# The h stage of the last 896 tokens with seven block products in place of eight

## The chip, the cores and the metric

The kernel runs on one core of a Trainium2 chip. The metric is the device time of one execution in microseconds; before the change it is 640.79 us, the median of three runs (639.9, 643.55, 640.79). PE is the matmul engine, DVE, ACT and POOL are the vector, scalar and GpSimd engines, SP issues the DMAs.

## The reference

Causal attention over 4 batches, 12 heads, 448 positions, head size 64, and on its output x (1792 tokens of 768) an MLP with a squared relu:

```python
scores = scale * np.matmul(q, k.transpose(0, 1, 3, 2))
scores = np.where(mask, -1000000000.0, scores)
attn = np.exp(scores - np.max(scores, axis=-1, keepdims=True))
attn = attn / (np.sum(attn, axis=-1, keepdims=True) + 1e-09)
x = (attn @ v).transpose(0, 2, 1, 3).reshape(B * S, H * D)
h = np.maximum(x @ w_in, 0.0)          # w_in  768 x 2048
return (h * h @ w_out)                 # w_out 2048 x 768
```

The weights arrive as 8-byte words, and everything else as f32.

## The kernel before, in words

Tokens are worked off in two halves of 896 (two batches each, `ph` 0 and 1). For a half, the 2048 columns of h are taken in four groups (`gr`) of four blocks of 128 (`GF`). A group has an h stage and an o stage. The h stage has eight units (`h_unit`, block f, batch h of the half): 6 blocks c of the 768 inputs, and for each of them three matmuls of 128 x 128 weights by 448 tokens, since every operand is held as a high and a low half (f32r) and hi*hi + hi*lo + lo*hi is summed in PSUM (lines 490 to 492). ACT then applies the relu from PSUM into a tile `r`, the square is taken, and `split` makes its two halves g (lines 240 to 250). The o stage has 14 units (`o_unit`, 7 token blocks by 2 column halves) of 4 x 3 matmuls of 384 columns (lines 526 to 528), added by DVE to `acc`; after the last group SP stores `acc` to the output (line 544).

Weights come in pieces (`piece`), 6 of w_in and 8 of w_out per group and half: SP loads 8-byte words into one of three `raw` tiles (line 467), two ACT, a shift, an addition and a combining instruction on DVE (lines 475, 243, 478) make an f32 in a `z` tile, and `split` writes a high half (ACT or POOL) and a low half (DVE or POOL) into `wi` or `wo`. All of this is done in both halves of the tokens.

Attention runs per pair of heads, 12 pairs for each half of the tokens (`attention`): scores (line 327), a masked maximum on DVE (340), exp on ACT (344), normalisation on POOL (353), transposes (367) and the product with v (387) on PE. The pairs of the second half of the tokens run between the MLP matmuls of the first half; their result goes to `x_dram` (line 435), and in the last o stage of the first half `again` loads the twelve blocks back (591) and splits them into the x tiles.

The order of the work is written by a planner (`Plan`). Every piece of work is an `op` with a rank, the engines that could do it with an assumed duration, what it reads and writes, and the buffers that it takes and drops. `emit` simulates the engines: it picks again and again the op that could start first (the rank decides between equals), and writes the instructions in the order of their simulated start. So each engine, and SP's DMA queue, has one fixed order; in the run an instruction waits for its data and buffers, and all behind it on that engine wait with it.

## Time and profile before

| what | value |
|---|---|
| median of three runs | 640.79 us (639.9 to 643.55) |
| profiled execution, span from first to last instruction | 638.4 us |
| what the median has above that span | 2.39 us |
| PE busy | 619.2 us (97%) |
| DVE, POOL, ACT busy | 450.4 (71%), 395.8 (62%), 356.7 us (56%) |
| DMA | 78.61 MB, mean 123 GB/s |

The profile is of one execution, whose time outside the span is not shown. "Busy" of PE adds up matmuls whose modelled ends overlap the next start, so a matmul's cost is read from the distance between starts. Engine names stand before lines of the kernel (L526 is line 526); operations recorded in a helper have the helper's line, so that tiles tell them apart.

### The profile page before, as it was taken

How to read it: one execution, taken by the hardware profiler on the slowest of the kernel's cores; microseconds unless marked ns; L12 is line 12 of the kernel's file. 1: busy time of each engine (PE TensorE's matmuls, PEld its weight loads, DVE VectorE, ACT ScalarE, POOL GpSimd, SP SyncE). 2: the span in 40 equal slices, each digit the busy share in tenths (PEclk: the TensorE clock that was granted, in tenths of full speed). 3: DMA queues.
4: the chain of work that ended last, by engine and by line, in shares of the span. 5: the costliest groups of instructions: out<-in, count | busy, mean ns of one | idle time of the engine just before them, and what ended most of it. 6: DMA issues, size and time to landing. Idle time of an engine off the chain costs nothing.

```text
span 638.4 us, 11482 instructions
## 1 busy us (share of the span) xinstructions
PE 619.2 (97%) x3936; PEld 544.8 (85%) x3936; DVE 450.4 (71%) x911; ACT 356.7 (56%) x856; POOL 395.8 (62%) x498
## 2 busy tenths in 40 slices
PE   3999999999999999999999999999999999999997
PEld 2666777798888898789888889999999999999997
DVE  5789865686668787678885479759845993897022
ACT  4789977676787456675557553545653344333300
POOL 1567854775678655767576688876657556656410
PEclk9799999999999999999999999999999999999999
DMA  9898931545574546544463258723541453141022
GB/s 156 158 201 150 186 80 31 109 154 152 118 173 130 151 98 155 152 96 115 126 159 100 77 164 248 210 73 109 158 130 34 108 155 101 59 123 50 1 87 87
DMA packets 134779, 78.61 MB, mean 123 GB/s; under 512 B 113729, under 2 KB 120385, under 8 KB 134721
## 3 DMA queue, kind: packets, MB, share of 16 engines
q1 hardware_dynamic: 131008, 77.42, 47.2%
q10 hardware_dynamic: 3712, 0.46, 0.5%
q8 instruction: 31, 0.51, 0.3%
q14 instruction: 28, 0.22, 0.1%
HBM read 69.60 MB, written 8.26 MB: 122 GB/s over the span
## 4 chain that ended last, share of the span: by engine, by line
PE 84%; DVE 5%; DMA 3%; POOL 3%; ACT 2%; issue 1%; SPq 0%; DVEq 0%; POOLq 0%; ACTq 0%
PE ps L526 12%; PE ps L527 12%; PE ps L528 12%; PE ps L490 11%; PE ps L491 11%; PE ps L492 11%; PE ps L387 6%; PE ps L367 5%; PE ps L327 4%; POOL ap L353 3%; DVE ps L340 2%; DMA v<-in_v_dram 1%; DMA bq<-in_q_dram 1%; ACT ap L344 1%; DMA aq<-in_q_dram 1%
## 5 line engine op out<-in xcount | busy, mean ns | idle before, releaser
L526 PE MATMUL ps<-wo,g 128*128 128x384 f32 x448 | 153.2, 342 | 0.0
L527 PE MATMUL ps<-wo,g 128*128 128x384 f32 x448 | 151.2, 338 | 0.0
L528 PE MATMUL ps<-wo,g 128*128 128x384 f32 x448 | 151.2, 337 | 0.0
L490 PE MATMUL ps<-x,wi 128*128 128x448 f32 x384 | 145.0, 378 | 0.6 <-ACT x L240 0.6
L491 PE MATMUL ps<-x,wi 128*128 128x448 f32 x384 | 140.6, 366 | 0.2 <-DVE x L243 0.2
L492 PE MATMUL ps<-x,wi 128*128 128x448 f32 x384 | 140.5, 366 | 0.0
L240 ACT ACTIVATE b<-raw 128x384 int32<-128x384 uint32 (+1 forms) x112 | 68.3, 610 | 89.1 <-DVE z L243 80.3
L243 DVE CUSTOM_DVE_ANT_0 z<-z,b 128x768 uint16<-128x768 uint16 (+1 forms) x112 | 102.9, 919 | 8.8 <-ACT b L240 1.9
L478 DVE SCALAR_TENSOR_TENSOR z<-raw,z 128x384 int32<-128x384 int32 (+1 forms) x112 | 94.8, 846 | 2.9
L353 POOL TENSOR_SCALAR ap<-ap,asm 128x448 f32<-128x448 f32 (+6 forms) x123 | 71.5, 600 | 35.1 <-DVE asm L411 21.8
L340 DVE CUSTOM_DVE_ANT_0 ps<-ps,mask 128x448 f32<-128x448 f32 (+6 forms) x168 | 68.8, 443 | 33.9 <-PE ps L327 24.9
L240 ACT ACTIVATE z<-raw 128x384 f32<-128x384 f32 (+1 forms) x112 | 67.8, 609 | 32.6 <-POOL wi L247 15.6
L526 PEld LDWEIGHTS ps<-wo,g 128*128 128x128 f32 x448 | 84.2, 188 | 1.4 <-issue 1.0
L527 PEld LDWEIGHTS ps<-wo,g 128*128 128x128 f32 x448 | 84.2, 188 | 0.1
L528 PEld LDWEIGHTS ps<-wo,g 128*128 128x128 f32 x448 | 84.1, 188 | 0.0
L490 PEld LDWEIGHTS ps<-x,wi 128*128 128x128 f32 x384 | 72.2, 188 | 9.0 <-issue 1.7
L475 DVE TENSOR_SCALAR z<-z 128x384 int32<-128x384 int32 (+1 forms) x112 | 63.3, 565 | 23.3 <-ACT z L240 23.0
L243 DVE TENSOR_TENSOR acc<-ps,acc 128x384 f32<-128x384 f32 x84 | 46.0, 550 | 46.1 <-PE ps L528 45.8
L492 PEld LDWEIGHTS ps<-x,wi 128*128 128x128 f32 x384 | 72.1, 188 | 6.1
L491 PEld LDWEIGHTS ps<-x,wi 128*128 128x128 f32 x384 | 72.2, 188 | 5.8 <-DVE x L243 0.5
L344 ACT ACTIVATE ap<-ps,mx 128x448 f32<-128x448 f32 (+6 forms) x126 | 58.7, 481 | 14.3 <-DVE mx L340 13.9
L247 POOL TENSOR_TENSOR g<-r,g 128x448 fp32r<-128x448 f32 x52 | 64.9, 1249 | 2.4
(65 smaller groups left out, 848.3 us busy)
## 6 DMA issues: line engine op xcount, KB each, us to landing
raw<-in_moe_w_in_dram SPq DMA_DIRECT2D x48, 512.0 KB, 3.9
raw<-in_moe_w_out_dram SPq DMA_DIRECT2D x64, 384.0 KB, 3.4
out_dram<-acc SPq DMA_DIRECT2D x28, 192.0 KB, 2.5
v<-in_v_dram SPq DMA_DIRECT2D x24, 192.0 KB, 4.0
ak<-in_k_dram SPq DMA_DIRECT2D x72, 56.0 KB, 2.7
aq<-in_q_dram SPq DMA_DIRECT2D x68, 56.0 KB, 2.6
x_dram<-xs SPq DMA_DIRECT2D x12, 224.0 KB, 3.8
xs<-x_dram SPq DMA_DIRECT2D x12, 224.0 KB, 2.7
```

The source lines that it names most:

```text
L240: return (ACT, t_act(n, psum, more), lambda: nc.scalar.activation(dst(), src(), func, **kw))
L243: return (DVE, t_dve(n) + more, lambda: nc.vector.tensor_tensor(out=dst(), in0=a(), in1=b(), op=op))
L340: plan.op(at, [(DVE, t_dve(w), lambda: nc.vector.tensor_tensor_reduce(out=at_(), in0=at_(), in1=mask[:, S - w:], scale=-SCALE, scalar=3.0e ...
L344: plan.op(at, [(ACT, t_act(w, True, 0.5), lambda: nc.scalar.activation(probabilities(c), at_(), AF.Exp, bias=mx.t, scale=-1.0, accum_out=s ...
L353: (POOL, 0.0005 * CW[c] + 0.34, lambda: nc.gpsimd.tensor_scalar(*operands(), 1.0, op0=ALU.mult, op1=ALU.mult)),
L478: plan.op(rank - 2, [(DVE, t_dve(n) + 0.2, lambda: nc.vector.scalar_tensor_tensor(out=z(), in0=word(1), scalar=-2 ** 31, in1=z(), op0=ALU. ...
L490: nc.tensor.matmul(o, w[:, 0], x[:, 0], start=c == 0, stop=False)
L491: nc.tensor.matmul(o, w[:, 0], x[:, 1], start=False, stop=False)
L492: nc.tensor.matmul(o, w[:, 1], x[:, 0], start=False, stop=c == NP - 1)
L526: nc.tensor.matmul(res(), g[:, 0], w[:, 0], start=f == 0, stop=False)
L527: nc.tensor.matmul(res(), g[:, 0], w[:, 1], start=False, stop=False)
L528: nc.tensor.matmul(res(), g[:, 1], w[:, 0], start=False, stop=f == GF - 1)
```

## The change

In the second half of the tokens the h stage is computed by Strassen's scheme. The weights of two blocks f1, f2 are cut in two along the 768 inputs (3 blocks each), and x in two along the inputs and in two by batch, so that h of the pair is a product of 2 x 2 blocks. Seven products (`SEVEN`) of sums of weight blocks by sums of x blocks (`OTHER`), each 3 x 3 matmuls of 448 columns, take the place of eight. Four PSUM banks a to d take them; some are accumulated on a second time after their first content was read, and four additions on DVE and the relus give the four blocks of h.

For this, x is no longer loaded back block by block: `x_parts` loads for each of three blocks four x blocks, makes four sums or differences and splits seven operands. Nine of the 21 operand tiles lie where the attention's buffers were (`replace` closes these), twelve are the x tiles. `w_parts` does the same for the weights of a pair: four blocks are read, added up from their halves, combined into s1 to s4, and the four sums are split again.

The weights of the second half are not converted anew: in the first half `keep` writes each converted piece's two halves into `wi_split` or `wo_split` in DRAM, from SP, and in the second half `w_parts` and `fetch` read them back. There is a third `z` tile. The three raw tiles, z and b lie in one tile that is lent out as f32 buffers when the last piece is converted. The twelve attention pairs of the second half run in another order (`turns`).

```diff
+    NRAW, NZ, NB, NR = 3, 3, 1, 6
+    CB = NP // 2
+    CBW = CB * P
...
+    words = const.tile([P, (NRAW + (NZ + NB) // 2) * PCW], I64, name="words")
+    whole = words.bitcast(I32)
+    plan.pool("raw", [words[:, i * PCW:(i + 1) * PCW] for i in range(NRAW)])
+    half = [whole[:, (2 * NRAW + i) * PCW:(2 * NRAW + i + 1) * PCW] for i in range(NZ + NB)]
+    plan.pool("z", half[:NZ])
+    plan.pool("b", half[NZ:])
+    plan.pool("r", tiles("r", NR, [P, S], F32), r=2, xs=2, y=6)
+    plan.pool("f", [], fz=5, s=3, xp=4)
+    spare = [whole[:, i * S:(i + 1) * S].bitcast(F32) for i in range((2 * NRAW + NZ + NB) * PCW // S)]
+    lent_f = plan.lend("f", spare)
+    NX = 9
+    wide = wi_t.rearrange("p i c f -> p (i c f)")
+    lent_w = plan.lend("w", [
+        wide[:, i * 2 * CBW:(i + 1) * 2 * CBW].rearrange("p (i c f) -> p i c f", i=2, c=CB)
+        for i in range(2 * GF)] + [lambda i=i: late["w"][i] for i in range(2)])
...
+    plan.pool("ps", tiles("ps", 8, [P, 512], F32, psum), mm=2, sc=4, pt=2, av=1, st=5)
...
+    def keep(rank, kind, gr, a, ch, after):
+        if kind == "i":
+            def go():
+                for i in range(2):
+                    nc.sync.dma_start(
+                        out=wi_dram[gr, :, a // CB, :, i, a % CB].rearrange("f p n -> p f n"),
+                        in_=wi_t[:, i, a].bitcast(F32).rearrange("p (f n) -> p f n", n=P))
+            plan.op(rank, [(DMA, 1.9, go)], [(("wi", a), 0), (("wi", a), 1)], [("wid", gr, a)], after)
+            return
+        plan.op(rank, [(DMA, 1.7, lambda: nc.sync.dma_start(
+            out=wo_dram[gr, a + GF * ch], in_=wo_part(a, ch)))],
+            [(("wo", a, ch), 0), (("wo", a, ch), 1)], [("wod", gr, a, ch)])
+
+    def fetch(rank, gr, a, ch):
+        plan.op(rank, [(DMA, 1.7, lambda: nc.sync.dma_start(
+            out=wo_part(a, ch), in_=wo_dram[gr, a + GF * ch]))],
+            [("wod", gr, a, ch)], [(("wo", a, ch), 0), (("wo", a, ch), 1)])
...
+    SEVEN = ("11", "s2", "12", "s3", "s1", "22", "s4")
+    OTHER = {"11": "11", "12": "21", "s4": "22", "22": "t4", "s1": "t1", "s2": "t2", "s3": "t3"}
+    x7, owned = {}, {}
+
+    def combine(rank, n, dst, a, b, op, reads, writes, **kw):
+        def of(h):
+            return lambda: h.t[:, :n]
+        plan.op(rank, [on_dve(n, of(dst), of(a), of(b), op), on_pool(n, of(dst), of(a), of(b), op)],
+                reads, writes, **kw)
+
+    def x_parts(i, rank, after):
+
+        B = {}
+        for m, (key, n) in enumerate((("11", i), ("12", NP + i), ("22", NP + CB + i), ("21", CB + i))):
+            B[key] = h = Hold("f", "xp")
+            plan.op(rank - 6 + m, [(DMA, 0.9, lambda h=h, n=n: nc.sync.dma_start(out=h.t, in_=x_dram[n]))],
+                    [("xd", n)], [h], take=h)
+
+        def done(key):
+            t = x7[key, i]
+            split(rank, S, lambda: t()[:, 0], lambda: t()[:, 1], lambda: B[key].t, [B[key]],
+                  ("x7", key, i), [after[owned[key, i]]], [B[key]])
+        B["t1"], B["t2"] = Hold("r", "xs"), Hold("r", "xs")
+        combine(rank, S, B["t1"], B["12"], B["11"], ALU.subtract, [B["12"], B["11"]], [B["t1"]],
+                after=[attended], take=B["t1"], drop=[B["11"]])
+        done("11")
+        combine(rank, S, B["t2"], B["22"], B["t1"], ALU.subtract, [B["22"], B["t1"]], [B["t2"]],
+                take=B["t2"], drop=[B["t1"], B["22"]])
+        done("t2")
+        done("21")
+        B["t3"] = B["12"]
+        combine(rank, S, B["12"], B["22"], B["12"], ALU.subtract, [B["22"]], [B["12"]],
+                drop=[B["22"]])
+        done("t3")
+        done("t1")
+        B["t4"] = B["21"]
+        combine(rank, S, B["21"], B["21"], B["t2"], ALU.subtract, [B["t2"]], [B["21"]],
+                drop=[B["t2"]])
+        done("t4")
+        done("22")
...
+    def w_parts(gr, u, rank, last):
+
+        Z, W, gate = {}, {}, list(ahead)
...
+        def whole(key, hi, lo, reads, drop):
+            Z[key] = z = Hold("f", "fz")
+            plan.op(rank, [
+                (DVE, t_dve(CBW) + 0.4, lambda: nc.vector.tensor_tensor(
+                    out=z.t[:, :CBW], in0=hi(), in1=lo(), op=ALU.add)),
+                (POOL, t_pool(CBW, True), lambda: nc.gpsimd.tensor_tensor(
+                    out=z.t[:, :CBW], in0=hi(), in1=lo(), op=ALU.add))],
+                reads, [z], take=z, drop=drop)
+
+        def fetched(m, f, j):
+            src = wi_dram[gr, 2 * u + f, j]
+            return (rank - 10 + m, src, [("wid", gr, CB * j + c) for c in range(CB)])
+
+        for m, (key, f, j) in enumerate((("11", 0, 0), ("22", 1, 1), ("12", 0, 1))):
+            W[key] = w = Hold("w", "w")
+            r, src, saved = fetched(m, f, j)
+            plan.op(r, [(DMA, 1.2, lambda w=w, src=src: nc.sync.dma_start(out=w.t.bitcast(F32), in_=src))],
+                    saved, [(w, 0), (w, 1)], gate, take=w)
+            whole(key, lambda w=w: flat(w.t[:, 0].bitcast(F32)), lambda w=w: flat(w.t[:, 1].bitcast(F32)),
+                  [(w, 0), (w, 1)], [w])
+        pair = [Hold("f", "fz"), Hold("f", "fz")]
+        r, src, saved = fetched(3, 1, 0)
+        for i, h in enumerate(pair):
+            plan.op(r, [(DMA, 0.7, lambda h=h, i=i: nc.sync.dma_start(
+                out=h.t[:, :CBW].rearrange("p (c n) -> p c n", n=P), in_=src[:, i]))], saved, [h], gate, take=h)
+        Z["21"] = pair[0]
+        combine(rank, CBW, pair[0], pair[0], pair[1], ALU.add, [pair[1]], [pair[0]], drop=[pair[1]])
+        Z["s1"], Z["s2"], Z["s4"] = Hold("f", "s"), Hold("f", "s"), Hold("f", "s")
+        Z["s3"] = Z["21"]
+
+        def done(key):
+            W[key] = w = Hold("w", "w")
+            split(at(key), CBW, lambda: flat(w.t[:, 0]), lambda: flat(w.t[:, 1]), lambda: Z[key].t[:, :CBW],
+                  [Z[key]], w, (), [Z[key]], take=w)
+
+        def made(key, a, b, op, drop):
+            combine(rank, CBW, Z[key], Z[a], Z[b], op, [Z[a], Z[b]], [Z[key]],
+                    take=Z[key] if key != "s3" else None, drop=[Z[d] for d in drop])
+        made("s1", "21", "22", ALU.add, ("22",))
+        made("s2", "s1", "11", ALU.subtract, ("s1", "11"))
+        done("s2")
+        made("s3", "11", "21", ALU.subtract, ("11",))
+        done("s3")
+        done("s1")
+        made("s4", "12", "s2", ALU.subtract, ("12", "s2"))
+        done("s4")
+        ahead[:] = plan.ops[-2:]
...
+    def h_pair(u, W, rank, step):
+
+        bank = {k: Hold("ps", "st") for k in "abcd"}
+        y = {k: Hold("r", "y") for k in ("u2", "u3", "11", "12", "21")}
+        f1, f2 = 2 * u, 2 * u + 1
+
+        def product(key, b, begin):
+            nonlocal rank
+            ps, w = bank[b], W[key]
+            for c in range(CB):
+                def go(c=c):
+                    x, o = x7[OTHER[key], c](), ps.t[:, :S]
+                    nc.tensor.matmul(o, w.t[:, 0, c], x[:, 0], start=begin and c == 0, stop=False,
+                                     skip_group_check=True)
+                    nc.tensor.matmul(o, w.t[:, 0, c], x[:, 1], start=False, stop=False,
+                                     skip_group_check=True)
+                    nc.tensor.matmul(o, w.t[:, 1, c], x[:, 0], start=False, stop=c == CB - 1,
+                                     skip_group_check=True)
+                plan.op(rank, [(PE, 3 * t_mm(S), go)],
+                        [(w, 0), (w, 1)] + [(("x7", OTHER[key], c), i) for i in range(2)], [ps],
+                        take=ps if begin and c == 0 else None, drop=[w])
+                rank += step
+
+        def out(b):
+            return lambda: bank[b].t[:, :S]
+
+        def add(k, b, a, take, drop):
+            plan.op(rank, [on_dve(S, lambda: y[k].t, out(b), lambda: y[a].t, ALU.add)],
+                    [bank[b], y[a]], [y[k]], take=y[k] if take else None, drop=drop)
+
+        def relu(k):
+            plan.op(rank, [on_act(S, lambda: y[k].t, lambda: y[k].t, func=AF.Relu),
+                           (DVE, t_dve(S, True), lambda: nc.vector.tensor_scalar(
+                               y[k].t, y[k].t, 0.0, None, op0=ALU.max))], [], [y[k]])
+
+        product("11", "a", True)
+        plan.op(rank, [on_act(S, lambda: y["u2"].t, out("a"), True)], [bank["a"]], [y["u2"]], take=y["u2"])
+        product("s2", "b", True)
+        add("u2", "b", "u2", False, [bank["b"]])
+        product("12", "a", False)
+        plan.op(rank, [on_act(S, lambda: y["11"].t, out("a"), True, AF.Relu)], [bank["a"]], [y["11"]],
+                take=y["11"], drop=[bank["a"]])
+        squared(f1, 0, y["11"], rank)
+        product("s3", "d", True)
+        add("u3", "d", "u2", True, [])
+        product("s1", "c", True)
+        add("u3", "c", "u3", False, [])
+        relu("u3")
+        squared(f2, 1, y["u3"], rank)
+        product("22", "d", False)
+        add("21", "d", "u2", True, [bank["d"], y["u2"]])
+        relu("21")
+        squared(f2, 0, y["21"], rank)
+        product("s4", "c", False)
+        add("12", "c", "u2", True, [bank["c"], y["u2"]])
+        relu("12")
+        squared(f1, 1, y["12"], rank)
...
     def group(ph, gr, rank, step, begin):
 
-        for c in range(NP):
-            piece(begin + (rank - begin) * (c + 0.5) / NP, "i", gr, c, 0, ())
+        if ph == 0:
+            for c in range(NP):
+                at = begin + (rank - begin) * (c + 0.5) / NP
+                piece(at, "i", gr, c, 0, ())
+                keep(at + 4, "i", gr, c, 0, swap)
+        else:
+            mid = (begin + rank) / 2
+            W = [w_parts(gr, 0, begin, mid), w_parts(gr, 1, mid, rank)]
...
+            for u in range(2):
+                rank = h_pair(u, W[u], rank, H_US * step)
         for i in range(2 * GF):
-            piece(begin + (rank - begin) * (i + 0.5) / 8, "o", gr, i % GF, i // GF, swap)
+            at = begin + (rank - begin) * (i + 0.5) / 8
+            if ph == 0:
+                piece(at, "o", gr, i % GF, i // GF, swap)
+                keep(at + 2, "o", gr, i % GF, i // GF, ())
+            else:
+                fetch(at, gr, i % GF, i // GF)
...
-    def again(n, at):
-        xs = Hold("xs", "xs")
-        plan.op(at - 6, [(DMA, 0.7, lambda: nc.sync.dma_start(out=xs.t, in_=x_dram[n]))],
-                [("xd", n)], [xs], take=xs, clear=[(("x", n), 0), (("x", n), 1)])
-        split(at, S, lambda: x_t[n][:, 0], lambda: x_t[n][:, 1], lambda: xs.t, [xs], ("x", n),
-              drop=[xs])
-
     rank, begin = start, 10.0
     rest = NG * (2 * GF * NP * H_US + 2 * NT * GF * O_US) - GF * NP * H_US
     for gr in range(NG):
         begin, rank = group(0, gr, rank, (rest + NA * 7.0) / rest, begin)
-    for n in range(NA, 2 * NA):
-        attention(even, n, start + (n - NA) * (rank - start - 30) / NA)
-    for n in range(NA):
-        again(n, begin + (rank - begin) * (n + 0.5) / NA)
+    mark = len(plan.ops)
+    turns = [NA + NP * b + CB * g + i for g in range(2) for b in range(2) for i in range(CB)]
+    for i, n in enumerate(turns):
+        attention(even, n, start + i * (rank - start - 30) / NA)
+
+    def over(ops, drop, go=lambda: None):
+        return plan.op(0.0, [(POOL, 0.0, go)], after=ops, drop=drop)
+
+    def replace():
+        early.close()
+        pool = ctx.enter_context(tc.tile_pool(name="second", bufs=1, side="right", reuse_waits="tile"))
+        late["x"] = tiles("x2_", NX, [P, 2, S], F32R, pool)
+        late["w"] = tiles("w2_", 2, [P, 2, CB, P], F32R, pool)
+
+    attended = over(plan.ops[mark:], lent_w[2 * GF:], replace)
+    over(pieces, lent_f)
+    entered = over(h_ops, lent_w[:2 * GF])
+    keys = [(key, i) for key in ("11", "t2", "21", "t3", "t1", "t4", "22") for i in range(CB)]
+    for i, key in enumerate(sorted(keys, key=lambda k: k[1])):
+        x7[key] = ((lambda i=i: late["x"][i]) if i < NX else (lambda i=i: x_t[i - NX]))
+        owned[key] = i >= NX
+    for i in range(CB):
+        x_parts(i, begin + (rank - begin) * (i + 0.5) / CB, [attended, entered])
```

## Rows read from the trace of the kernel before

**Rows 1.** Page: busy of PE; then the clock that was granted, in 40 slices

```profile
PE 619.2 (97%) x3936; PEld 544.8 (85%) x3936; DVE 450.4 (71%) x911; ACT 356.7 (56%) x856; POOL 395.8 (62%) x498
...
PEclk9799999999999999999999999999999999999999
```

**Rows 2.** Page: the chain that ended last, share of the span by engine

```profile
PE 84%; DVE 5%; DMA 3%; POOL 3%; ACT 2%; issue 1%; SPq 0%; DVEq 0%; POOLq 0%; ACTq 0%
```

**Rows 3.** PE's waits, 110 to 364.4, then 364.4 to 638.4: us, times, longest

```profile
PE ps L367 <- POOL ap L353: 1.0, 2, 0.8
...
PE ps L367 <- POOL ap L353: 1.1, 3, 0.5
```

**Rows 4.** Windows: us; busy PE, PEld, DVE, ACT, POOL; clock; DMA share; GB/s

```profile
110.00:364.40 254.40, 252.45 (x1662) 219.66 (x1661) 186.60 (x394) 163.10 (x403) 169.43 (x206) 1.00 0.50 129
...
364.40:399.90 35.50, 34.45 (x202) 32.45 (x201) 30.55 (x43) 17.21 (x32) 30.68 (x31) 1.00 0.67 201
...
376.00:399.80 23.80, 23.80 (x137) 23.80 (x136) 22.53 (x32) 10.14 (x18) 19.44 (x18) 1.00 0.78 229
...
390.00:395.00 5.00, 5.00 (x31) 5.00 (x30) 3.90 (x7) 1.53 (x3) 4.17 (x6) 1.00 0.95 265
```

**Rows 5.** Timeline of PE, first matmul of stages in the second half: start, duration

```profile
399.76 0.36 PE L490 MATMUL ps<-x,wi 128*128 128x448 f32 x1
...
428.95 0.34 PE L526 MATMUL ps<-wo,g 128*128 128x384 f32 x1
...
458.07 0.37 PE L490 MATMUL ps<-x,wi 128*128 128x448 f32 x1
...
487.83 0.34 PE L526 MATMUL ps<-wo,g 128*128 128x384 f32 x1
```

**Rows 6.** Timelines of POOL and PE about the end of the last attention pair

```profile
361.97 1.15 POOL L247 TENSOR_TENSOR x<-xs,x 128x448 fp32r<-128x448 f32 x1
...
364.59 5.40 POOL L353 TENSOR_SCALAR ap<-ap,asm 128x64 f32<-128x64 f32 x7 [0.43 <-ACT r L240]
...
364.38 0.34 PE L526 MATMUL ps<-wo,g 128*128 128x384 f32 x1
...
373.40 1.95 PE L387 MATMUL ps<-apt,v 128*64 128x448 f32 x16
```

**Rows 7.** Tiles acc, x and g: duration ns shortest/median/longest, first and last start

```profile
L243 DVE TENSOR_TENSOR acc<-ps,acc x84: 506/550/560, 206.7 to 634.9; 128x384 f32<-128x384 f32 x84
...
L243 DVE TENSOR_TENSOR x<-ps,x x12: 584/620/625, 27.5 to 113.8; 128x448 fp32r<-128x448 f32 x12
...
L247 POOL TENSOR_TENSOR g<-r,g x52: 1131/1157/1657, 77.3 to 607.7; 128x448 fp32r<-128x448 f32 x52
L250 POOL TENSOR_SCALAR g<-r x49: 553/569/999, 75.6 to 607.1; 128x448 fp32r<-128x448 f32 x49
...
L243 DVE TENSOR_TENSOR g<-r,g x12: 610/1426/2757, 118.8 to 545.9; 128x448 fp32r<-128x448 f32 x12
```

**Rows 8.** Page: DMA issues, count, KB each, median us to landing

```profile
xs<-x_dram SPq DMA_DIRECT2D x12, 224.0 KB, 2.7
```

**Rows 9.** Lines by shape (busy us, mean ns), then POOL's timeline

```profile
L240 ACT ACTIVATE r<-ps 128x448 f32<-128x448 f32 x64 | 34.9, 546 | 55.7 <-PE ps L492 55.0 <-POOL g L247 0.5
...
L240 ACT ACTIVATE r<-r 128x448 f32<-128x448 f32 x43 | 24.8, 577 | 1.1
...
L247 POOL TENSOR_TENSOR r<-r 128x448 f32<-128x448 f32 x21 | 21.2, 1012 | 30.0 <-ACT r L240 30.0
...
356.70 0.57 POOL L250 TENSOR_SCALAR g<-r 128x448 fp32r<-128x448 f32 x1 [4.02 <-ACT r L240]
357.35 1.13 POOL L247 TENSOR_TENSOR g<-r,g 128x448 fp32r<-128x448 f32 x1
```

**Rows 10.** Waits of SP's queue, 110 to 364.4, then all: us, times, longest

```profile
SPq L467 <- DVE z L478: 135.2, 42, 7.7
...
SPq L591 <- POOL x L247: 11.8, 5, 4.3
```

110 lines of the change are left out of this document (68 added, 42 removed).

## The prediction

> **What bounds the kernel now.** I read the page's first two parts first. PE is busy 97% of the span, its granted clock is full speed from the third slice on, and the other engines stand between 56% and 71% [rows 1]. The chain of waits says the same in another way: 84% of the time that set the end is PE work, and what is left (DVE, DMA, POOL, ACT) lies almost wholly in the first 110 us, where attention starts up [rows 2]. Next come PE's own waits: from 110 us to the end the only releaser that PE waits for at length is POOL's L353, the softmax normalisation, 1.0 us before 364.4 and 1.1 us after it, and the waits after it all fall before 371; from there on PE waits for nothing [rows 3]. The windows agree: 252.45 busy of 254.40 us, then 34.45 of 35.50 [rows 4]. So the part that the diff rewrites, the second 896 tokens, runs at the pace of PE alone, and an instruction taken from PE there is time taken from the end, as long as the rest keeps up.
>
> **What a matmul of the h stage costs.** The "busy" time of one matmul overlaps the next, so I take the distance of stage borders instead. The first h stage of the second half goes from 399.76 to 428.95, 29.19 us, the second from 458.07 to 487.83, 29.76 [rows 5]; there are four, and the third and fourth last as long as the first within 0.02 us. Each holds 4 x 2 x 6 x 3 = 144 matmuls of 448 columns, so the distance is 0.2027 us in three of them and 0.2067 in one; the mean is 0.2037. Each o stage holds 168 matmuls of 384 columns and is untouched: 458.07 - 428.95 = 29.12 us.
>
> **The change part by part.**
>
> *Fewer products.* A pair of f blocks took 8 block products of 9 matmuls, now 7. There are two pairs per group and four groups, so 8 x 9 = 72 matmuls go, 576 to 504. At 0.2037 us that is **-14.7 us** (-14.6 at the lower distance, -14.9 at the higher). Size, type and weight load of each matmul stay the same, so I keep the distance.
>
> The Trainium skill ("TensorE: Matmul & The Clock Gate", section "Wait — 56ns, not 53.3ns?") gives columns divided by 2.4 GHz plus about 2.5 ns for back-to-back matmuls. For 448 columns that makes 0.189 us, and the gain by it would be 13.6 us. The trace reads 0.2037, and the measurement decides.
>
> *The conversions of the second half go.* All 24 + 32 pieces of f64 words (two ACT, three DVE, two split instructions each) leave the second half. They were off PE's path there, so the gain is nothing. Their raw loads are replaced by read-backs of the same size (two f32 halves in place of 8 bytes), so DMA reads in the second half stay as they are.
>
> *The x operands, at the border of the halves.* This is the place that I fear most. Before, 12 splits were spread over the last o stage. Now each of three blocks of x needs 4 loads, 4 combinations and 7 splits: 12 combinations and 21 low halves, which are two-input instructions on DVE or POOL, and 21 high copies on ACT or POOL. Their tiles lie where the attention buffers were, so they start only after the last attention product, whose first matmul is at 373.40 and which ends at 375.35 [rows 6]. The first Strassen product is due at 399.76 [rows 5] and needs the first operand of all three blocks; one more operand is due every 9 x 0.2037 = 1.83 us, the seventh at 410.8. By 399.76 the first two blocks (22 two-input instructions) and two instructions of the third must be through, 24 in all, in 24.4 us. The weights' part for the first pair (8 combinations, 4 low halves) can start when the last h stage's weights are free, at 364.4 [rows 6], so I count it as done beside the attention's tail, although POOL runs the last normalisation there until 370 [rows 6]. The second pair's 8 combinations do compete.
>
> Price of one: a two-input DVE instruction on SBUF takes 0.61 us at its shortest, but the median of the split of g is 1.43 and the longest 2.76, while one whose other input is in PSUM stays between 0.51 and 0.56 (acc) or 0.58 and 0.63 (x). POOL takes 1.16 [rows 7]. So the DVE instruction is held while POOL works: half a dozen of these pairs cost about the sum of both, not the larger. Lower bound of the wait: both engines in parallel, 1/0.61 + 1/1.16 = 2.5 instructions per us, 24 in 9.6 us: no wait. Upper bound: strictly in turn, and all eight combinations of the second pair ahead, 16 x 0.61 + 16 x 1.16 = 28.3 us, a dozen high copies on POOL at 0.57 = 6.8, and two load gaps of 2.7 (a block's buffers come free late, and a load of x lands after 2.7 us [rows 8]) = 5.4: 40.5 us, so 375.35 + 40.5 = 415.9, **16 us** late. I take turns, half of the second pair's eight ahead, four copies on POOL, one load gap: 12 x 0.61 + 12 x 1.16 + 4 x 0.89 + 4 x 0.57 + 2.7 = 29.8, end at 405.1, **+5 us**. That is nearer to the in-turn rows because the medians of g are; ACT can take the copies, idle 13.7 of 23.8 us in this stretch [rows 4]. What stood there before filled DVE 22.5 and POOL 19.4 of the same 23.8 us, so there was little air.
>
> The Trainium skill ("SBUF — State Buffer", section "Who interferes with whom") says that a DVE instruction with two SBUF inputs and a POOL instruction that reads SBUF exclude each other for a whole instruction. The trace agrees (2.76 us against 0.61). Taken strictly it gives the upper bound above, which is a rival below.
>
> *Inside the second half's h stages.* Bank a is accumulated on again by product 12 after ACT has copied it (0.55 us, [rows 9]) under the 1.83 us of product s2; banks d and c are read by DVE (0.62, x from PSUM in [rows 7]) under one product each. Nothing there. DVE and POOL have per group 24 two-input instructions for weights and at most 16 for squares and low halves, about 40 x 0.89 = 36 us in turn, of a group of some 55: enough air. At the change to the o stage the last g is late: after product 22, one addition 0.62, relu 0.58, square 1.01, copy 0.57, low half 1.16 and four hand-overs that I estimate at 0.1 each (the copy of g that ends at 357.27 is followed by its low half at 357.35) = 4.3 us [rows 7, 9]. It is covered by product s4 (1.83) and by those nine matmuls of the first and of the second o unit that don't need it (2 x 9 x 0.173 = 3.1): 4.9. If only the first unit stands ahead, 0.9 us open per group, 3.5 in all; I take 0.3 per group, **+1.2 us**.
>
> *The first half.* 48 writes of 256 KB and 32 of 384 KB are added on SP's queue, 25 MB, from about 110 us on. DMA was at a share of 0.50 from 110 to 364; 265 GB/s took 0.95 [rows 4], so 25 MB take 25.2/265 x 0.95 = 90 us of all engines in about 290, and the share goes to about 0.8. SP issues 80 more at about 0.33 us, 27 us; it spent 135 us of that stretch waiting for raw buffers [rows 10], so the issue fits in. The new wait is SP's: a write waits for the low half of its piece, and raw, q, k and v loads queue behind it. Cost from below: -2.1 us, if the two waits of PE [rows 3] go (an x split stands on POOL just ahead of the last normalisation, at 361.97 [rows 6], and moves away); from above: a write's wait as SP already has it for a low half on POOL, 11.8 us in five times, 2.4 each, longest 4.3 [rows 10], times 56 pieces, 132 us on SP, of which PE sees what exceeds its loads' lead. I take **-0.5 us**: three raw buffers and loads one attention turn ahead hide the waits, and one of the two PE waits goes.
>
> **Sum.** 638.4 - 14.7 + 5 + 1.2 - 0.5 = 629.4 us of span. The median of the runs (640.8) is 2.4 above the profiled span; I take that as what lies around it: **631.8 us**, 1.4% faster.
>
> **Rivals.**
>
> 1. *The border eats it.* DVE and POOL strictly in turn, 16 us late: 640.8 - 14.7 + 16 + 1.2 = 643.3; from 10 us late on it is 637 or more. For it: the held DVE instructions, and DVE and POOL already 42 of 47.6 us busy there. Against: a product needs only one more operand every 1.83 us, and ACT takes copies. Chance 0.12.
> 2. *Slower: SP in order.* Each of the 56 writes keeps SP until its low half is done; a raw or q load behind it comes late, a conversion comes late, and the fixed order of PE's list waits for it. It decides from (14.7 - 6.2 + 0.5) / 56 = 0.16 us of PE time per piece; at 0.5 us it costs 28: 640.8 - 14.7 + 6.2 + 28 = 660. For it: the waits of 2.4 us and a DMA share of 0.8. Against: PE waited 0 us for a DMA after 110 us, and SP's long waits there cost nothing. Chance 0.10.
> 3. *All of it comes.* No wait at the border or before o, and PE's two waits go: 640.8 - 14.9 - 2.1 = 623.8. Chance 0.12.
> 4. *The products do not get fewer in time:* every h stage at 0.2067 in place of 0.2027, 504 x 0.004 = 2 us less gain. That moves the likeliest case within its range and has no chance of its own.
>
> **How the numbers follow.** The likeliest case (0.66) has 0 to 10 us at the border and 0 to 3.5 before o: 626 to 637.5. With 0.12 below that (to 623.8) and 0.12 above (637 to 643) and 0.10 at 644 to 660, a range of 624.5 to 642 leaves out about 0.2. A difference of 0.5%, 3.2 us, is what the runs can tell from none (they spread from 639.9 to 643.55): faster 0.78 (the likeliest and the third), same 0.12 (the first), slower 0.10 (the second).
>
> **What would show it.** Right: 504 matmuls of 448 columns in the second half; its four h stages some 25.6 us each in place of 29.3; a gap or slow start of PE at about 400 whose releaser is a DVE or POOL x instruction; gaps of under 1 us before each o stage. PE's start of the second half at 399 to 405. Wrong: new PE waits between 110 and 364 with a chain that goes through SP's writes; h stages of 28 us or more, with PE waiting for DVE inside a pair.

## Result, and the profile after

The changed kernel took 633.91 us (median of four runs, 631.81 to 634.98), the kernel before beside it 642.17 (639.9 to 644.45): the ratio is 0.9865, 95% interval 0.9833 to 0.9898. The forecast was 631.8. The profiled execution took 634.02 us with a span of 632.1, so 1.9 lie around the span.

The page after, its busy row, clock and chain, stands against [rows 1, 2]: 3864 matmuls, 72 fewer, and PE's share of the chain falls from 84% to 76% while DVE's rises from 5% to 11%. PE is still the bound, but more of the path is now spent waiting for the elementwise engines.

```profile
PE 606.5 (96%) x3864; PEld 529.6 (84%) x3864; DVE 377.7 (60%) x825; ACT 319.2 (50%) x790; POOL 377.7 (60%) x464
...
PEclk9799999999999999999999999999999999999999
...
PE 76%; DVE 11%; POOL 5%; DMA 3%; ACT 2%; issue 2%; ACTq 0%; DVEq 0%; POOLq 0%
...
wi_split<-wi SPq DMA_DIRECT2D x48, 256.0 KB, 3.7
wo_split<-wo SPq DMA_DIRECT2D x32, 384.0 KB, 4.0
```

PE's timeline after, the first matmul of the stages of the second half (start, duration), answers [rows 5]. It has a new pattern: after the first 18 matmuls of an o stage (464.11 less 434.33 holds 171 matmuls, not 168) PE does the first three matmuls of the next group's h stage and then the other 150 of o.

```profile
404.39 0.37 PE L690 MATMUL ps<-x,wi 128*128 128x448 f32 x1
...
434.33 0.34 PE L751 MATMUL ps<-wo,g 128*128 128x384 f32 x1
...
464.11 0.37 PE L690 MATMUL ps<-x,wi 128*128 128x448 f32 x1
...
489.30 0.33 PE L751 MATMUL ps<-wo,g 128*128 128x384 f32 x1
...
519.09 0.37 PE L690 MATMUL ps<-x,wi 128*128 128x448 f32 x1
...
544.21 0.33 PE L751 MATMUL ps<-wo,g 128*128 128x384 f32 x1
```

From these rows the second half can be laid beside the one before. Its first h stage (126 matmuls in place of 144) lasts 434.33 - 404.39 = 29.94 us. The other three last 25.80, 25.73 and 25.78 with the three matmuls done ahead, a distance of 0.2045 each; four of 25.77 would be 103.1. Before they summed to 117.3. So the missing matmuls gave 14.2 us, and the first stage lost 4.2 of it. The four o stages went from 117.8 to 116.8. From the first h matmul to the end of the last matmul the time fell from 235.1 to 224.1 us: **11.0 gained**. But the second half starts at 404.39 and not at 399.76: **4.6 lost ahead of it**. The last matmul ends 6.4 us earlier (634.84, then 628.48).

Not all of the 4.6 can be put down to the change. The first o matmul of the first half stands in both kernels behind the same amount of PE work; here it is, before and then after.

```profile
126.82 0.34 PE L526 MATMUL ps<-wo,g 128*128 128x384 f32 x1
...
128.78 0.33 PE L751 MATMUL ps<-wo,g 128*128 128x384 f32 x1
```

So 2.0 us are lost in the start-up, and 2.7 from that mark to the second half (272.94, then 275.61). Six of the profiles below have the same order on PE up to the end of the last attention product. In them the first o matmul starts anywhere from 126.1 to 127.7; from it to that end they and the one here all take 250.5 to 250.7 us, against 248.5 before. The 2.7 are steady. The 2.0 lie within what the start-up varies by from profile to profile, and no run shows that the change causes them.

PE's waits say where the two losses are. Columns: us in total, times, longest. The first row is one of 0 to 110 us that the kernel before does not have. The second is that of 110 to 404 and answers both rows of [rows 3], whose later waits all fall before 371. The last two are those of 404 to the end and have no counterpart before.

```profile
PE ps L355 <- ACT bpt L283: 2.3, 1, 2.3
...
PE ps L395 <- POOL ap L381: 4.3, 9, 1.0
...
PE ps L692 <- DVE x L286: 1.6, 2, 1.2
PE ps L690 <- ACT r L283: 1.4, 1, 1.4
```

Behind 404 it is the border, as feared: x operands (DVE), and the copy of bank a out of PSUM (ACT r). Ahead of 404 it is the softmax normalisation on POOL, L381 here and L353 before: 2.1 us in five waits have become 4.3 in nine. And there is a new wait in the start-up, at 46 us, ahead of the first write to `wi_split` (120.5 us). The windows (us; busy PE, PEld, DVE, ACT, POOL; clock; DMA share; GB/s) agree: PE was idle 1.95 us in the 254.4 of [rows 4], and is now 4.5 in 250.

```profile
110.00:360.00 250.00, 245.50 (x1608) 212.27 (x1607) 177.99 (x380) 157.13 (x386) 161.20 (x194) 1.00 0.79 223
...
404.39:434.33 29.94, 26.86 (x127) 23.34 (x127) 23.04 (x27) 14.55 (x28) 28.75 (x28) 1.00 0.58 185
464.11:489.30 25.19, 25.19 (x124) 23.01 (x124) 11.68 (x17) 11.07 (x21) 19.53 (x22) 1.00 0.46 145
```

The second of these rows is the first h stage: PE lacks 3.1 us, and POOL works 28.75 of 29.94 us. The other 1.1 of the 4.2 us stand in longer distances next to the waits and, 0.4 of them, in one gap at 431.9. In the next group's stage PE lacks nothing.

How the border looks on the engines: the timeline of the kernel after, rows of PE, then ACT, DVE and POOL (start, duration, and in brackets the wait and its releaser).

```profile
406.38 0.47 PE L692 MATMUL ps<-x,wi 128*128 128x448 f32 x1 [0.39 <-DVE x L286]
...
410.92 0.47 PE L690 MATMUL ps<-x,wi 128*128 128x448 f32 x1 [1.41 <-ACT r L283]
...
413.17 0.47 PE L692 MATMUL ps<-x,wi 128*128 128x448 f32 x1 [1.18 <-DVE x L286]
...
404.99 0.58 ACT L283 ACTIVATE x<-words 128x448 fp32r<-128x448 f32 x1 [4.75 <-DVE words L286]
407.84 0.58 ACT L283 ACTIVATE x<-r 128x448 fp32r<-128x448 f32 x1 [2.27 <-DVE r L286]
...
410.34 0.53 ACT L283 ACTIVATE r<-ps 128x448 f32<-128x448 f32 x1
...
404.88 1.44 DVE L286 TENSOR_TENSOR x<-words,x 128x448 fp32r<-128x448 f32 x1
...
408.73 0.55 DVE L286 TENSOR_TENSOR acc<-ps,acc 128x384 f32<-128x384 f32 x1
409.20 1.11 DVE L286 TENSOR_TENSOR x<-r,x 128x448 fp32r<-128x448 f32 x1
410.23 1.55 DVE L286 TENSOR_TENSOR x<-words,x 128x448 fp32r<-128x448 f32 x1
411.71 1.41 DVE L286 TENSOR_TENSOR x<-r,x 128x448 fp32r<-128x448 f32 x1
413.04 1.57 DVE L286 TENSOR_TENSOR x<-words,x 128x448 fp32r<-128x448 f32 x1
...
409.78 1.52 POOL L290 TENSOR_TENSOR x<-words,x 128x448 fp32r<-128x448 f32 x1
411.26 1.38 POOL L290 TENSOR_TENSOR wi<-words,wi 128x384 fp32r<-128x384 f32 x1
412.60 1.53 POOL L290 TENSOR_TENSOR words<-words,r 128x448 f32<-128x448 f32 x1
```

The DVE rows with both inputs in SBUF last 1.1 to 1.6 us, most of them about as long as the POOL row beside them; the row with one input in PSUM (acc) keeps its 0.55 among them. The first wait ends with the low half that DVE writes from 404.88 to 406.32, the last operand of the first product. The second ends with ACT's copy of bank a: the first product is through by 407.1, but the copy stands on ACT behind high halves of x and of a weight, which came late from DVE, and starts at 410.34. The third is a low half of x again.

### The profile page after: what moved, and what is told of

Same layout as the page of the kernel before. It is cut to its first block, busy times and chain, and to the rows that moved or that the text cites. A ratio compares the mean times of both kernels' runs of the same rounds, so it can differ in the third digit from the quotient of the medians.

```text
span 632.1 us, 11245 instructions
## 1 busy us (share of the span) xinstructions
PE 606.5 (96%) x3864; PEld 529.6 (84%) x3864; DVE 377.7 (60%) x825; ACT 319.2 (50%) x790; POOL 377.7 (60%) x464
## 4 chain that ended last, share of the span: by engine, by line
PE 76%; DVE 11%; POOL 5%; DMA 3%; ACT 2%; issue 2%; ACTq 0%; DVEq 0%; POOLq 0%
PE ps L751 11%; PE ps L753 11%; PE ps L752 11%; PE ps L395 6%; PE ps L415 6%; PE ps L692 5%; PE ps L690 5%; PE ps L694 5%; PE ps L355 5%; PE ps L556 4%; PE ps L558 4%; PE ps L557 4%; POOL ap L381 4%; DVE words L286 2%; DVE words L532 2%
## 5 line engine op out<-in xcount | busy, mean ns | idle before, releaser
L381 POOL TENSOR_SCALAR ap<-ap,asm 128x448 f32<-128x448 f32 (+6 forms) x119 | 67.7, 588 | 55.7 <-DVE asm L439 32.5
L283 ACT ACTIVATE r<-ps 128x448 f32<-128x448 f32 x60 | 32.7, 546 | 107.7 <-PE ps L694 80.3
L283 ACT ACTIVATE words<-words 128x384 f32<-128x384 f32 (+2 forms) x112 | 65.0, 614 | 33.2 <-DMA words<-in_moe_w_out_dram 15.6
L556 PE MATMUL ps<-x,wi 128*128 128x448 f32 x192 | 74.3, 387 | 0.0
L558 PE MATMUL ps<-x,wi 128*128 128x448 f32 x192 | 70.3, 366 | 0.0
L557 PE MATMUL ps<-x,wi 128*128 128x448 f32 x192 | 70.2, 366 | 0.0
L293 POOL TENSOR_SCALAR wi<-words 128x512 fp32r<-128x512 f32 (+1 forms) x29 | 17.4, 601 | 83.0 <-PE ps L692 58.3
L286 DVE TENSOR_TENSOR r<-ps,r 128x448 f32<-128x448 f32 x40 | 24.9, 622 | 69.6 <-PE ps L694 68.4
L290 POOL TENSOR_TENSOR g<-r,g 128x448 fp32r<-128x448 f32 x45 | 55.8, 1241 | 4.1 <-ACT g L283 1.7
L290 POOL TENSOR_TENSOR wi<-words,wi 128x512 fp32r<-128x512 f32 (+1 forms) x44 | 55.2, 1258 | 2.9 <-ACT wi L283 1.3
L283 ACT ACTIVATE r<-r 128x448 f32<-128x448 f32 x72 | 41.6, 578 | 23.3 <-DVE r L286 21.0
L286 DVE CUSTOM_DVE_ANT_0 words<-words 128x768 uint16<-128x768 uint16 (+1 forms) x56 | 47.6, 849 | 9.2 <-ACT words L283 4.1
L395 PE MATMUL ps<-ident,ap 128*128 128x128 f32 x288 | 44.8, 287 | 8.5 <-POOL ap L381 7.8
```

Source lines behind the costliest of these rows:

```text
L283: return (ACT, t_act(n, psum, more), lambda: nc.scalar.activation(dst(), src(), func, **kw))
L286: return (DVE, t_dve(n) + more, lambda: nc.vector.tensor_tensor(out=dst(), in0=a(), in1=b(), op=op))
L290: lambda: nc.gpsimd.tensor_tensor(out=dst(), in0=a(), in1=b(), op=op))
L381: (POOL, 0.0005 * CW[c] + 0.34, lambda: nc.gpsimd.tensor_scalar(*operands(), 1.0, op0=ALU.mult, op1=ALU.mult)),
L395: nc.tensor.transpose(ps.t[:, n * P:(n + 1) * P], s.p[:, POFF[c] + kc * P:POFF[c] + (kc + 1) * P], ident[:, o:o + P])
L556: nc.tensor.matmul(o, w[:, 0], x[:, 0], start=c == 0, stop=False)
```

## Experiments

Each is set against the kernel before, run beside it on the same chip; where two kernels that ran on different chips are compared, the difference is that of their ratios, times 641 us. "Attention's end" is the end of the last attention product: 375.28 us in the trace before, 379.32 after.

**The changed kernel again**, for its own interval beside the others.

> The changed kernel once more, beside the other kernels of this chip. Both theories expect what was seen: about 634 us, 1.3% below before; second half from about 404, its first h stage (with the three matmuls that stand behind the first o units) some 30.5 us and the other three 25.8. If the late start of the second half (404.4 against 399.8) was chance of one profile, this profile starts it near 400.

633.79 us, ratio 0.9891 [0.9874, 0.9907]. The profile repeats the one above (waits of 0.39, 1.40 and 1.17 at the border; attention's end at 378.28), but for the granted clock, 0.89 from 404 to 420 in place of 1.00, which makes the first h stage 31.17 us. The first o matmul starts at 127.71, 1.1 earlier than in the first profile, and attention ends 1.0 earlier by it. The kernels below are held against this one.

**Eight products.** One product more per pair, so 576 matmuls again; the added one repeats another, so the h it yields is not the reference's.

```diff
         product("s4", "c", False)
+        product("11", "b", False)
```

> An eighth product of nine matmuls per pair is put back (the first product is added once more on the bank of the second; h is wrong by it), all else stays. Theory (PE alone sets the pace of the second half, the matmul count is the gain): 72 more matmuls at 0.2037 us, 12.9 to 14.7 us more than the changed kernel (less than the full sum since the border's late operands get one product more of time), so 646 to 649, about 1% above before; each of the last three h stages goes from 25.8 to 29.4. Rival (the shorter h stages already wait for the weights' and additions' work, and the extra product fills waits): under 8 us more.

646.69 us, 1.0093 [1.0078, 1.0109]: 12.9 us over the changed kernel. The three h stages behind the border last 29.4 us each (3 or 6 matmuls ahead, then 28.77, 28.17, 28.18) against 25.8. So a product removed is worth its 9 x 0.2 us in full; in the first stage, 32.86 us, the added product covers part of the wait and costs less. This kernel also shows what the rest of the change costs by itself: with the matmuls of before it is 0.9% slower than before.

**Where the weights' combinations stand.** The second pair of weights is combined only once the x operands are made.

```diff
-            W = [w_parts(gr, 0, begin, mid), w_parts(gr, 1, mid, rank)]
+            W = [w_parts(gr, 0, begin, mid), w_parts(gr, 1, mid, rank, made_x if gr == 0 else ())]
...
+    made_x = plan.ops[-1:]
```

> The eight combinations for the second pair's weights of the first group wait until the last x operand is made; nothing else is changed, and the first half has the same order on PE. Theory (DVE and POOL take turns, so what bounds the border is the sum of all two-input work ahead): these eight stood between 391 and 406 on POOL and DVE with some 1.3 us each, so the x operands come about 5 us earlier, the waits of PE for DVE x and ACT r at 406 to 413 go, the first h stage falls from 30.5 to about 26.5, with perhaps 1 to 2 us of a new wait at the second pair, and the time is 2 to 4 us below the changed kernel. Rival (the border is bound by the loads of x and SP's order): the waits stay, the first h stage stays at 30 or is longer because the second pair's weights come late too, and the time is the same or 2 to 4 us higher.

631.63 us, 0.9858 [0.9839, 0.9877], 2.2 less than the changed kernel beside it. The first h stage lasts 28.88 us, against 29.94 and 31.17 in the two profiles of the changed kernel, the longer one at the clock of 0.89. One wait for x is left, and one for the products' additions comes in its place: the timeline of PE in this kernel.

```profile
409.90 0.47 PE L692 MATMUL ps<-x,wi 128*128 128x448 f32 x1 [1.79 <-DVE x L286]
...
416.10 0.48 PE L690 MATMUL ps<-x,wi 128*128 128x448 f32 x1 [0.63 <-DVE r L286]
```

So the combinations ahead are a part of the border's cost, 1.1 us of the 4.2 by the profiles at full clock, 2.2 by the runs, and not all of it; a stage of 26.5 us was expected.

**All combinations and low halves of the second half on DVE, high halves on ACT.** POOL keeps only the squares and the splits of g.

```diff
-        plan.op(rank, [on_dve(n, of(dst), of(a), of(b), op), on_pool(n, of(dst), of(a), of(b), op)],
+        plan.op(rank, [on_dve(n, of(dst), of(a), of(b), op)],
...
-        plan.op(rank, [copy_on_pool(n, hi, src), on_act(n, hi, src)],
+        plan.op(rank, [on_act(n, hi, src)] if alone else [copy_on_pool(n, hi, src), on_act(n, hi, src)],
```

> All combinations and low halves for x and for the weights of the second half run on DVE alone, their high copies on ACT alone; POOL has only squares and halves of g there. Theory (turns): a two-input DVE instruction falls from 1.0 to 1.6 us at the border to about 0.61, so 33 x 0.61 + 20 x 0.55 + 11 x 0.55 = 37 us of DVE for all of x and both pairs' weights, from 369 on; the first h stage falls to 26 or 27 and the time by 3 to 4 us. Rival (two engines side by side do more than one): the 53 instructions on one engine take as long as 53 x 1.2 / 2 did on two only if each halves; if they stay at 1 us or more, the border wait grows by 10 us or more and the time by as much.

633.01 us, 0.9878 [0.9857, 0.9899]: 0.8 less than the changed kernel, inside both intervals, where 3 to 4 were expected. Lines by shape of the two kernels from 376 to 420 us (busy us, mean ns) show what the engines do to each other. First the changed kernel, in its second profile, in which both engines work:

```profile
L286 DVE TENSOR_TENSOR x<-words,x 128x448 fp32r<-128x448 f32 x9 | 10.5, 1164 | 0.0
L290 POOL TENSOR_TENSOR x<-words,x 128x448 fp32r<-128x448 f32 x6 | 8.8, 1467 | 0.0
...
L286 DVE TENSOR_TENSOR x<-r,x 128x448 fp32r<-128x448 f32 x4 | 5.5, 1383 | 0.0
```

Then DVE alone:

```profile
L286 DVE TENSOR_TENSOR x<-words,x 128x448 fp32r<-128x448 f32 x15 | 9.1, 616 | 0.0
...
L286 DVE TENSOR_TENSOR x<-r,x 128x448 fp32r<-128x448 f32 x6 | 3.6, 617 | 0.0
```

Fifteen low halves took 19.3 us of two engines' time together, and take 9.1 of one alone; and DVE's share of it, nine, took longer beside POOL (10.5) than all fifteen without. One engine by itself makes the operands sooner than both: the last low half of x is done 31.1 us after attention's end, and 36.4 in the changed kernel. The Trainium skill ("SBUF — State Buffer", section "Who interferes with whom") says that a DVE instruction with two inputs in SBUF and a POOL instruction that reads SBUF shut each other out; the rows agree, 1164 to 1383 ns beside POOL and 616 alone. At the border PE now waits 0.2 us. But PE's waits from 362 us on in this kernel, and a row of DVE just ahead of the first, show where the gain went:

```profile
PE ps L688 <- DVE r L286: 3.5, 2, 1.8
PE ps L690 <- DVE x L286: 0.2, 1, 0.2
...
477.36 4.61 DVE L286 TENSOR_TENSOR words<-words 128x384 f32<-128x384 f32 x5
```

They fall at 483.0 and 539.9, inside later h stages: combinations of weights stand on DVE ahead of the additions that free a bank, and with no POOL to share them PE waits for the bank. 3.5 us came back.

**DVE alone at the border only.** The same, but in the later groups the planner may use both engines for the weights again.

```diff
-        combine(rank, CBW, pair[0], pair[0], pair[1], ALU.add, [pair[1]], [pair[0]], drop=[pair[1]])
+        combine(rank, CBW, pair[0], pair[0], pair[1], ALU.add, [pair[1]], [pair[0]], drop=[pair[1]], alone=gr == 0)
```

> As dve_alone, but only for the x operands and for the weights of the first group of the second half; the later groups share the work between DVE and POOL as in the change. Theory (in turns at the border; later groups lose if DVE has it all, as dve_alone waited 1.85 and 1.62 us for DVE r in the second and third group): the border keeps dve_alone's gain (first group 3.5 us shorter than in the changed kernel), the later h stages are 25.8 again, and the time is 3 to 4 us below the changed kernel, 630. Rival (the gain at the border came from o units that the planner moved into the waits, and the later waits are paid anyway): 632 to 634.

629.40 us, 0.9823 [0.9806, 0.9841]: 4.4 us less than the changed kernel. All that PE waits from 362 us to the end:

```profile
PE ps L693 <- DVE x L286: 0.2, 1, 0.2
PE ps L691 <- DVE r L286: 0.2, 1, 0.2
```

From attention's end to the last matmul it takes 245.96 us, the changed kernel 249.16 and 250.64 in its two profiles (the longer one with the clock of 0.89), the kernel before 259.56. So with POOL kept out of the operands 3.2 us of the border's 4.2 are gone by the profiles. The runs differ by 4.4, which holds more than the border.

The kernel differs in a second thing, though: the planner gave PE another order at the border. The first h matmul is at 385.26, and o matmuls stand between the products. That order could cover waits by itself, as the rival had it. What DVE makes tells the two apart as far as it goes: the last low half of x, in the changed kernel and here (attention's end 379.32 and 376.83).

```profile
415.07 0.61 DVE L286 TENSOR_TENSOR x<-words,x 128x448 fp32r<-128x448 f32 x1
...
407.37 0.61 DVE L286 TENSOR_TENSOR x<-words,x 128x448 fp32r<-128x448 f32 x1
```

It is done 36.4 us after attention's end there and 31.2 here. An estimate from these traces: with PE's order of the changed kernel and no waits, the last low half of the second product would be due 28.3 us after attention's end (25.07 to the first product, 16 matmuls of 0.2045). Here it is done after 28.1, and the later operands have more to spare. So by this estimate the mutual hold of DVE and POOL accounts for the waits for x at the border. The changed kernel's order of PE with DVE alone was not run.

**The first half: is it the traffic?** The writes of groups 1 to 3 are left out, and the reads take the place of group 0, so the output of the last 896 tokens is not the reference's. The planner still sees all writes.

```diff
-                for i in range(2):
+                for i in range(2 if gr == 0 else 0):
...
-        plan.op(rank, [(DMA, 1.7, lambda: nc.sync.dma_start(
+        plan.op(rank, [(DMA, 1.7, lambda: gr or nc.sync.dma_start(
```

> Only the first group's weights are written to DRAM, and the second half reads these for every group; the order of all other work stays, on PE exactly. 60 of 80 writes go from SP and 19 of 25 MB. Theory (the 4.6 us by which the second half starts later come from the writes, through SP's order and the DMA share of 0.9): PE's waits for POOL ap between 160 and 320 (4.3 us) shrink to below 1.5, and the second half starts 2 to 4 us earlier, at 400 to 402. Rival (they come from the new order alone, through the third z tile and the other attention order): nothing moves, the start stays at 404 and the waits stay.

633.16 us, 0.9876 [0.986, 0.9892], 0.6 less than with all writes. The window from 110 to 360 of this kernel:

```profile
110.00:360.00 250.00, 245.43 (x1602) 212.12 (x1601) 176.44 (x371) 155.06 (x381) 163.49 (x195) 1.00 0.56 147
```

The DMA share goes back from 0.79 to 0.56, nearly that of before, and PE is as idle as with all the writes, with the same nine waits of 4.3 us for POOL. From the first o matmul to the second half it takes 275.71 us, against 275.61. So in this order of the work the traffic of groups 1 to 3 is not the cause.

**The kernel before with the writes.** Only the 80 writes are added, in the planner's list and on the queue; nothing reads them.

```diff
+            if ph == 0:
+                keep(at + 4, "i", gr, c, 0, swap)
```

> The kernel before with the 80 writes of the converted weights to DRAM added in the first half, planned as in the change; nothing reads them, and the second half is the old one. Theory (the first half's loss of some 3.6 us belongs to the writes with their place in the plan, and z2 and quarter_writes moved nothing since they leave that plan): 2.5 to 4.5 us above before, second half from 402 to 404. Rival (it belongs to the other edits: tile pools, the attention order, the x and weight work planned into the last o stage): within 1 us of before, second half from about 400.

**The same, with writes that move nothing:** the planner places them and counts their DMA time, but issues none.

```diff
-        plan.op(rank, [(DMA, 1.7, lambda: nc.sync.dma_start(
-            out=wo_dram[gr, a + GF * ch],
-            in_=late["wo"][:, :, a, ch * CH:(ch + 1) * CH].bitcast(F32)))],
+        plan.op(rank, [(DMA, 1.7, lambda: None)],
```

> As before_writes, but the writes stand in the plan only and are not issued: the order of all other work is that of before_writes. Theory (the order is the larger part of it, since three quarters of the DMA work left out saved 0.6 us): as late as before_writes within 1 us. Rival (SP's queue and the DMA traffic are the larger part): back at the time of before within 1 us.

644.57 us, 1.0063 [1.0046, 1.0081], and 645.94 us, 1.0077 [1.0057, 1.0096]. Both are 3.9 and 5.2 us slower than before (640.72), and the one that moves no byte isn't the faster one (1.4 us slower, a little more than the 1 us that was expected at most; the intervals overlap). PE's waits from 110 to 405 us in the kernel without bytes, and its window:

```profile
PE ps L367 <- POOL ap L353: 4.4, 12, 1.1
```

```profile
110.00:360.00 250.00, 245.72 (x1605) 212.24 (x1604) 187.03 (x382) 158.59 (x385) 159.43 (x198) 1.00 0.50 128
```

The DMA share is that of before and the waits for the normalisation are those of after. Attention's end is at 381.27 (with real writes 379.69), and from there on both take what before takes: 259.56 and 259.67 us. From the first o matmul to the second half, the start-up left out, before takes 272.94 us, the kernel without bytes 277.25, with real writes 276.10, and the changed kernel 275.61. So the order of the instructions, which the planner writes anew when it counts 80 more transfers on its model of the queue, is enough to cost what the first half lost, with no byte moved: PE, whose order is fixed, waits for POOL's normalisations twelve times instead of five. Which moved instruction makes a normalisation late was not followed up.

**The third z tile.** The change gives the conversions three z tiles; before had two. Here there are two again.

```diff
-    NRAW, NZ, NB, NR = 3, 3, 1, 6
+    NRAW, NZ, NB, NR = 3, 2, 2, 6
...
-    plan.pool("b", half[NZ:])
+    plan.pool("b", half[NZ:][:1])
```

> Two z tiles as before the change instead of three, all else of the change stays (its tile becomes a spare). The order on PE then equals that of the kernel before for the first 448 matmuls. Theory (the third z tile moved the start-up: more pieces loaded early, so PE waits about 2 us for ACT bpt at 44 us behind a weight load that took 7.5 us): that wait goes and 40 to 80 us has 38 us of PE work again in place of 36.3; the second half starts 1.5 to 2.5 us earlier, the time is 1 to 3 us below the changed kernel. Rival (start-up varies by chance): the wait stays or the time does not move.

632.91 us, 0.9885 [0.9866, 0.9903], 0.4 less than the changed kernel by the ratios, inside both intervals. The wait for bpt at 46 us is gone, but attention ends at 378.37 (378.28 in the second profile of the changed kernel), with 4.1 us of waits for POOL, and from the first o matmul to the second half it takes 275.55 us, as with three tiles. That wait also comes and goes with three z tiles: 2.3 and 1.8 us in the two profiles of the changed kernel, 0.2 in the one with a quarter of the writes. So no cost of the third tile is shown.

**As the last, with the writes at no cost in the planner**, so that it orders more of the first half as before (the order of PE is that of before for 1051 matmuls; in the trace the h and o matmuls follow it to 253 us).

```diff
-            plan.op(rank, [(DMA, 1.9, go)], [(("wi", a), 0), (("wi", a), 1)], [("wid", gr, a)], after)
+            plan.op(rank, [(DMA, 0.0, go)], [(("wi", a), 0), (("wi", a), 1)], [("wid", gr, a)], after)
```

> Two z tiles, and the planner counts the writes to DRAM at zero time on its DMA queue (they are issued all the same). The order on PE equals that of the kernel before for the first 1051 matmuls. Theory (what the first half lost is the new order that the planner made, since the planned writes fill its one DMA queue for about 100 us): the waits for POOL ap at 160 to 200 and 280 to 330 (4.3 us) fall to the 1 to 2 us of before, the second half starts at 399 to 401, and the time is 3 to 4 us below the changed kernel. Rival (writes that stand on SP where the plan didn't count them hold up loads): PE waits behind loads appear between 120 and 360 and the time is no better or worse.

639.74 us, 0.9986 [0.9972, 1.0]: slower than the last by 6.8. The old order does not bring the old time back: from the first o matmul to the second half it takes 279.99 us. Attention ends at 383.99; PE's waits from 110 to 405 us, and three windows of this kernel:

```profile
PE ps L395 <- POOL ap L381: 5.9, 7, 1.9
```

```profile
150.00:170.00 20.00, 17.29 (x109) 14.28 (x108) 13.10 (x31) 13.27 (x30) 11.19 (x14) 0.83 0.91 225
170.00:210.00 40.00, 40.00 (x263) 33.66 (x263) 28.68 (x58) 29.75 (x73) 30.94 (x37) 1.00 0.94 254
250.00:270.00 20.00, 16.79 (x96) 13.77 (x95) 11.61 (x32) 9.96 (x28) 10.00 (x14) 0.91 0.92 247
```

There are fewer waits than in the changed kernel, but longer ones, in stretches with a DMA share of 0.91 and 0.92, and the granted clock falls to 0.83 and 0.91 in them. The share by itself does not do it, since from 170 to 210 it is 0.94 and PE lacks nothing. So the writes are not free: the planner's new order costs 2.7 us in the changed kernel, and writes that the order does not count come to 7 us here. That an order made without the writes doesn't fit a queue that has them is a reading; which transfer is late I did not isolate, and the waits name POOL. It stays open.

**The border and the z tiles together:** the edits of two kernels above in one.

```diff
-    NRAW, NZ, NB, NR = 3, 3, 1, 6
+    NRAW, NZ, NB, NR = 3, 2, 2, 6
...
-        combine(rank, CBW, pair[0], pair[0], pair[1], ALU.add, [pair[1]], [pair[0]], drop=[pair[1]])
+        combine(rank, CBW, pair[0], pair[0], pair[1], ALU.add, [pair[1]], [pair[0]], drop=[pair[1]], alone=gr == 0)
```

> dve_border with two z tiles instead of three. If the 0.9 us that z2 lay below the changed kernel is real, this is 628.5; if it was noise, 629.4 like dve_border.

628.42 us, 0.9813 [0.9791, 0.9835], the lowest of all: 5.0 us less than the changed kernel, and by the ratios 0.6 less than DVE alone at the border with three z tiles, inside both intervals. So the runs do not tell whether the z tile adds anything. From attention's end to the last matmul 245.65 us, 13.9 less than before. Its attention ends at 377.37, 2.1 later than before.

## Why the prediction was right, and where it was not

The forecast of the total was right (631.8 against 633.91, in the likeliest case's own range of 626 to 637.5), and by its main steps; one term was wrong in sign, and two others came out better for reasons that the forecast did not have, which is luck. The time around the span was 1.9 us and not the 2.4 taken. In the order of the sum, span by span:

- *Fewer products, -14.7.* Measured -14.2: 504 matmuls at 0.2045 in place of 576 at 0.2037. The run with eight products confirms it from the other side: 18 matmuls cost 3.6 us per stage. The step of size, type and weight load staying the same holds.
- *The border, +5.* Measured +4.2, in the place and by the mechanism named: a first h stage of 29.94 us, with DVE and POOL instructions that hold each other. The operands of the first product were ready at 406.32, 27.0 us after attention's end; worked out were 29.8. The run with DVE alone there takes 3.2 of it away; by the estimate above the shorter low halves are enough for that without PE's new order. The one with later combinations shows that the second pair's weights ahead are a part. But the wait lies elsewhere than in the sum: ahead of the first product's last operand PE waits 0.4 us, and the rest inside the second and third product.
- *Inside the h stages, "nothing there".* Wrong for the first stage: the copy of bank a takes 0.53 us as priced, but ACT does it in order, behind the high halves, and PE waits 1.4 for it. I had counted the copy and not the queue that it stands in. It is within the +4.2. From the second stage on it holds.
- *Before the o stages, +1.2.* Measured 0. There is no wait: after 18 o matmuls the planner put three of the next group's h stage. I had the cover of 18 matmuls right and added 0.3 for the case that it didn't suffice.
- *o stages, no change.* Measured -0.9: two stages of before had a distance of 0.1767 and none after has (the four last 29.17 to 29.31). Not expected, and no run here explains it.
- *The first half, -0.5.* Measured **+4.6: the step that failed.** Of it 2.0 lie in the start-up, where the profiles vary by as much, and 2.7 behind it. What it says of DMA and SP held. The DMA share went to 0.79 as worked out (0.8). SP does wait for low halves, in the rows below of SP's queue from 110 to 404 us (us, times, longest; L483 and L478 are the writes), 34 us in 24 times (54 us at the writes with all other releasers), within my bound of 132, and PE waits for no transfer there. What I didn't price is that the kernel's order comes from a planner that counts these writes: every engine's list in the first half is another one. I looked for a cost in the added instructions and not in the moved ones. The kernel before with writes that move nothing loses 4.3 us on the same stretch.

```profile
SPq L483 <- POOL wo L290: 21.9, 15, 3.3
...
SPq L478 <- POOL wi L290: 12.5, 9, 4.4
```

A reading of the chain was wrong as well: what it holds besides PE does not lie almost wholly in the first 110 us. There it is 55 us, and 46 lie from 110 to 375, 11 of them POOL's normalisation; two of these pieces in the kernel before (start, us, and how many in a row):

```profile
253.16 2.03 POOL ap L353 x3
...
276.21 2.84 POOL ap L353 x4
```

So the path already ran through POOL where the changed kernel then lost time. Behind 375 the chain is PE's, as the forecast had it.

Summed: -14.2 + 4.2 - 0.9 + 4.6 = -6.3, the span's 638.4 - 632.1. The forecast had -9.0 by -14.7 + 5 + 1.2 - 0.5, and the 2.7 between are the first half's 5.1 and 0.5 less from the matmuls, against 0.8, 1.2 and 0.9 that came out better at the border, before the o stages and in them.

Of the rivals, the first (the border eats it) had the right mechanism at a quarter of its size. The second (SP in order) falls for the changed kernel, where taking three quarters of the writes away gains 0.6 us; where the planner does not count the writes, PE loses 7 us on the stretch behind the start-up. The third (all of it comes) is nearly reached from attention's end on by the best kernel, 13.9 us against the 14.2 of the matmuls, and by none ahead of it. The fourth, the distance, was 0.4 us in size.

## What to carry to other kernels

Where a planner writes the order, price a change also by what the planner will do to the parts that it does not touch: put the new operations in its list with nothing behind them, and compare. Compare from a mark behind the start-up, if that varies: here the start-up differed by up to 2.6 us between profiles of the same order, and the stretch behind it by 0.2. Where two engines hold each other on the same memory, count them in turn, and try one of them alone where the work is urgent; but only there, since the engine that works alone is late for the next thing. And find the bound of a saving by taking the saving back: the kernel with eight products gave the price of a product and that of the overhead in one run.
